# Chunked linear attention and a gated projection on one core: one visit of TensorE per unit, other PSUM banks, and signs by an AND

## The chip, the cores and the metric

The kernel runs on one core of a Trainium2 chip. The metric is device time in microseconds (us) from the start to the end of one execution. A core has TensorE (PE, with its weight load PEld), VectorE (DVE), ScalarE (ACT), GpSimd (POOL) and SyncE (SP), which issues the DMAs. A value that PE makes lands in one of eight PSUM banks.

## The reference

```python
def _attn_ref(q, k, v, alpha):                 # (4, 8, 768, 48)
    for t in range(S):
        state = alpha[:, :, t, :, None] * state + np.einsum('bhd,bhe->bhde', k[:, :, t], v[:, :, t])
        y[:, :, t] = np.einsum('bhd,bhde->bhe', q[:, :, t], state)
def _moe_ref(x, w_gate, w_val, w_out):         # x (3072, 384), d_ff 1536
    gate = 1.0 / (1.0 + np.exp(-(x @ w_gate)))
    return (gate * (x @ w_val) @ w_out)
```

A recurrence per batch and head with a decay per channel, and on its output, token by token, a sigmoid-gated two-matrix layer. All of it in float32.

## The kernel before, in words

**The dense part.** The 3072 tokens are six groups g of 512; each group takes 12 steps, one per 128 columns of the inner width, 72 steps s in all. To keep float32's accuracy a weight and an activation are each split into a high and a low part, and three products stand for one (`PAIRS`). A step has nine matmuls of 128x512 for the gate (into the bank `pg`), nine for the value (`pv`), and nine (`po`, three banks) which multiply the gated result of an earlier step by `w_out`: six with its high part `hh`, three with its low part `hl`. Between them ScalarE makes the sigmoid `sg` (L595), VectorE multiplies it into `pv` (L597), ScalarE casts that to `hh` (L599), and VectorE subtracts for `hl` (L600), which is the last reader of the `pv` bank.

**The attention part.** A unit u is one group of tokens and one pair of heads: 24 units, four per group. The first eight (`unit`) work in chunks of 128 tokens, the other sixteen (`late`) in chunks of 64. A late unit has on PE: four transposes of the decayed k (`turned`, L386, to `at`); the scores of 64x64 (`scores`, L526, two `at` banks); the products of k and v that are added to the state (`adds`, L533, the same two); and the outputs (`outputs`, L569, to `pg`). VectorE has two scans for the decays (L367, L371), the scaling of q (L515), the masks on the scores (L539, four per unit), eight state updates one after another (L552), and the subtract `yt` (L398) that splits the output; ScalarE copies the transposes to `kn` (L390) and casts the output (L397); GpSimd scales k (L374) and the states (`vs`, L557). The split output goes by DMA into `x`, the input of the next group's steps.

**The weights** come as 64-bit numbers and are cut into two float32 parts on the chip: for each of 25 pieces ScalarE scales the upper word (L333) and moves the top bits of the lower (L334), VectorE joins sign and bits by two `scalar_tensor_tensor` (L337), ScalarE casts (L339) and VectorE subtracts (L341). This and the eight early units fill the first part of the kernel.

**What sets the order.** `Plan` records every piece with its engine, an estimated time, a due step (`key`), and what it reads and writes; `order` then simulates the engines and takes, of the pieces that are ready, the one with the earliest due time. Instructions are issued in that order, engine by engine, and the tile framework adds the waits. Rings (`r_at`, `r_pg`, `r_pv`, `r_po`) hand out the banks in turn. For a late unit `begin` sets the due steps from `last_step`: transposes, scores, products and outputs have each their own.

Of the kernel before, what the change touches and what calls it, by code (L numbers as in the profile page):

```python
# [8 lines left out]
F32 = mybir.dt.float32  # L9
# [8 lines left out]
P = 128  # L18
# [206 lines left out]
def chunked(ctx, tc, rows, vc, vh, weights_in, out, const, ident, flags, weights, within):  # L225
# [67 lines left out]
    sb.tile([P, 104], F32, name="apart")  # L293
# [20 lines left out]
    plan.add("gpsimd", 1.5, NF - 4.0, later, writes=["later", *(("start", u) for u in range(EARLY))])  # L314
# [5 lines left out]
    def weight_piece(f, key):  # L320
        cuts = (0, DM, 2 * DM, WF) if f == 0 else (0, WF // 2, WF)
        over = before(f"w{f}") if f >= 6 else []
        for i, (lo, hi) in enumerate(zip(cuts, cuts[1:])):
# [4 lines left out]
            most = raw.bitcast(U16).rearrange("p m (w h) -> p m w h", h=2)[:, :, 0, 1]  # L328
# [83 lines left out]
    def unit(u, g, p, t):  # L412

        n, nch = T, CH
        bank = r_bank if u < NP else r_at
# [15 lines left out]
        (pkn, pk), *pas = bank.next(), bank.next(), bank.next()  # L431
# [47 lines left out]
        pyn, py = pas[0] if u < NP else r_pg.tiles[0]  # L479
# [15 lines left out]
    def late(u, g, p, t):  # L495
# [4 lines left out]
            out=tin[:, 0:A_Q], in_=rows[g, p, :, 0:A_Q]), writes=[(inn, m) for m in "ark"])  # L500
        (an, A), (vn, v), (vsn, vs) = r_A.next(), r_v.next(), r_vs.next()
        own = [slice(R * j, R * j + R) for j in range(2)]
        other = own[::-1]
        for j in range(2):
            plan.add("sync", (0.475, R * T * 4 / RATE), after(t["load"], 0.1), lambda j=j: nc.sync.dma_start(
                out=A[own[j], j], in_=rows[g, p, own[j], A_Q:WIDTH]), writes=[(an, 2 + j)])
        plan.add("sync", (0.475, P * CH * 2 * D * 4 / RATE), after(t["load"], 0.2), lambda: nc.sync.dma_start(
            out=v.rearrange("p c j e -> p (c j e)"), in_=vc[g, p]), writes=[(vn, "v")])
        for j in range(2):
            plan.add("sync", (0.475, R * EH * D * 4 / RATE), after(t["load"], 0.3), lambda j=j: nc.sync.dma_start(  # L510
                out=vs[other[j], j].rearrange("p c e -> p (c e)"), in_=vh[g, p, j]), writes=[(vsn, j)])
        kT = tin[:, A_K:A_Q]
        fn, F, decn, dec = decays(u, E, t, inn, tin)
# [4 lines left out]
        (pkn, pk), *pas = r_at.next(), r_at.next(), r_at.next()  # L518
# [111 lines left out]

    for i in range(WARM):
        warm(i)
# [192 lines left out]
```

## Time and profile before

| | us |
|---|---|
| median of 3 runs (lowest, highest) | 573.31 (571.58, 576.84) |
| the profiled execution | 573.71 |
| its span, first to last instruction | 571.6 |

The profile is of one execution. Times in its rows are from the start of the span; a large matmul's row (387 ns and more) overlaps the next one, so PE's pace is read from the chain of waits, where groups stand one behind another.

### The profile page before, as it was taken

The numbers are of one execution on the slowest core, as the hardware profiler recorded it, in microseconds if no ns is written. First come the engines' busy times: TensorE is split into PE (matmuls) and PEld (weight loads), VectorE is DVE, ScalarE is ACT, GpSimd is POOL, SyncE is SP. The second block draws the span as 40 slices with busy tenths as digits, with TensorE's granted clock in tenths as the row PEclk, the third lists the DMA queues.
The fourth block names the chain that finished last, engine by engine and source line by source line (L and its number), as shares of the span: only waits on it lengthen the run. The fifth ranks groups of instructions, "written<-read, shape, count | busy, mean of one in ns | idle before, by whom it ended". The sixth has DMA issues, their size and how long they took to land.

```text
span 571.6 us, 10275 instructions
## 1 busy us (share of the span) xinstructions
PE 553.7 (97%) x4150; PEld 434.1 (76%) x4150; DVE 335.2 (59%) x648; ACT 182.0 (32%) x331; POOL 93.3 (16%) x133
## 2 busy tenths in 40 slices
PE   8969999989999999999999999999999999999995
PEld 4657887767877777777777778777777878888884
DVE  7797989999753664754754844745748252221221
ACT  1556667653322222322212222213222212212121
POOL 6530212222210120220220210210202010000000
PEclk9988999999999999999999999999999999999999
DMA  8764775643412223312312332312332011100001
GB/s 316 255 190 154 249 214 177 192 140 106 153 49 79 60 74 84 122 56 80 90 52 61 112 108 60 106 57 61 92 127 61 1 29 29 55 1 0 3 0 60
DMA packets 21831, 55.90 MB, mean 98 GB/s; under 512 B 3472, under 2 KB 8592, under 8 KB 21776
## 3 DMA queue, kind: packets, MB, share of 16 engines
q1 hardware_dynamic: 21776, 55.17, 31.4%
q8 instruction: 34, 0.56, 0.4%
q14 instruction: 21, 0.17, 0.1%
HBM read 41.01 MB, written 4.72 MB: 80 GB/s over the span
## 4 chain that ended last, share of the span: by engine, by line
PE 89%; DVE 6%; issue 2%; DMA 1%; POOL 1%; ACT 0%; SPq 0%; DVEq 0%; POOLq 0%
PE pv L221 25%; PE po L608 25%; PE pg L221 25%; PE pg L569 3%; PE pv L580 2%; PE at L526 2%; PE at L386 1%; DMA x<-yt 1%; PE at L533 1%; PE at L438 1%; DVE st L552 1%; DVE raw L337 1%; DVE w L341 1%; DVE F L371 1%; PE pg L485 1%
## 5 line engine op out<-in xcount | busy, mean ns | idle before, releaser
L221 PE MATMUL pg<-x,w 128*128 128x512 f32 x648 | 162.8, 395 | 2.7 <-DMA x<-yt 2.7
L221 PE MATMUL pv<-x,w 128*128 128x512 f32 x648 | 162.2, 394 | 1.5 <-DVE hl L600 1.5
L221 PEld LDWEIGHTS pv<-x,w 128*128 128x128 f32 x648 | 120.1, 188 | 32.0 <-DVE hl L600 6.8
L221 PEld LDWEIGHTS pg<-x,w 128*128 128x128 f32 x648 | 120.5, 189 | 29.8 <-issue 3.1
L597 DVE TENSOR_TENSOR pv<-pv,sg 128x512 f32<-128x512 f32 x72 | 50.3, 699 | 122.2 <-PE pv L221 118.8
L608 PE MATMUL po<-hh,w 128*128 128x512 f32 x432 | 115.3, 395 | 0.1
L595 ACT ACTIVATE sg<-pg 128x512 f32<-128x512 f32 x72 | 43.1, 598 | 198.0 <-PE pg L221 108.2
L600 DVE TENSOR_TENSOR hl<-pv,hh 128x512 fp32r<-128x512 f32 x72 | 49.7, 690 | 84.5 <-PE po L608 69.9
L608 PEld LDWEIGHTS po<-hh,w 128*128 128x128 f32 x432 | 79.4, 188 | 16.6 <-ACT hh L599 0.5
L599 ACT CAST hh<-pv 128x512 fp32r<-128x512 f32 x72 | 42.1, 585 | 113.7 <-DVE pv L597 62.9
L608 PE MATMUL po<-hl,w 128*128 128x512 f32 x216 | 66.7, 406 | 0.0
L557 POOL TENSOR_TENSOR vs<-st,dec 64x384 f32<-64x384 f32 x32 | 26.9, 841 | 238.1 <-DVE st L552 218.2
L608 PEld LDWEIGHTS po<-hl,w 128*128 128x128 f32 x216 | 38.3, 188 | 8.5 <-issue 0.2
L374 POOL TENSOR_TENSOR in<-in,G 128x512 f32<-128x512 f32 x22 | 30.4, 1382 | 82.9 <-DVE G L367 30.3
L552 DVE SCALAR_TENSOR_TENSOR st<-st,dec,at 128x48 f32<-128x48 f32 x128 | 33.8, 264 | 7.9 <-PE at L533 2.9
L539 DVE TENSOR_TENSOR A<-at,mask 64x256 f32<-64x256 f32 x64 | 27.0, 422 | 1.5
L367 DVE TENSOR_TENSOR_SCAN G<-in,d1g 128x512 f32<-128x512 f32 x22 | 26.7, 1214 | 1.9 <-DMA in<-in_rows_dram 1.8
L371 DVE TENSOR_TENSOR_SCAN F<-in,d1f 128x512 f32<-128x512 f32 x22 | 27.6, 1253 | 0.1
L515 DVE TENSOR_TENSOR A<-A,F 64x512 f32<-64x512 f32 x32 | 22.7, 711 | 1.3 <-DMA A<-in_rows_dram 0.8
L569 PEld LDWEIGHTS pg<-A,vs 112*48 112x48 f32 (+1 forms) x512 | 16.8, 123 | 6.8 <-issue 6.8
L337 DVE SCALAR_TENSOR_TENSOR raw<-raw 128x576 uint32<-128x576 uint32 (+1 forms) x28 | 20.5, 747 | 0.0
L569 PE MATMUL pg<-A,vs 112*48 112x64 f32 (+1 forms) x512 | 18.8, 221 | 1.0 <-issue 0.4
(132 smaller groups left out, 391.1 us busy)
## 6 DMA issues: line engine op xcount, KB each, us to landing
in<-in_rows_dram SPq DMA_DIRECT2D x16, 516.5 KB, 3.7
raw<-in_w_dram SPq DMA_DIRECT2D x12, 576.0 KB, 4.6
x<-yt SPq DMA_DIRECT2D x35, 192.0 KB, 3.3
first_w<-in_w_dram SPq DMA_DIRECT2D x10, 576.0 KB, 4.7
out_dram<-raw SPq DMA_DIRECT2D x18, 256.0 KB, 2.5
v<-in_vc_dram SPq DMA_DIRECT2D x22, 192.0 KB, 3.5
A<-in_rows_dram SPq DMA_DIRECT2D x32, 128.0 KB, 2.7
in<-in_rows_dram SPq DMA_DIRECT2D x4, 772.5 KB, 5.0
```

Of the source, the lines that this page charges most:

```text
L221: nc.tensor.matmul(out=dst, lhsT=lhs(a, i), rhs=rhs(b, i), start=(n == 0 and i == 0), stop=(n == len(todo) - 1 and i == NK - 1))
L371: plan.add("vector", scan(n), after(t["G"], 0.01), lambda: nc.vector.tensor_tensor_scan(out=F, data0=az[:, 0:n], data1=d1f, initial=0.0, o ...
L374: plan.add("gpsimd", pool_(n), t["kt"], lambda: nc.gpsimd.tensor_tensor(out=kT, in0=kT, in1=G, op=ALU.mult), [gn, (inn, "r")], [(inn, "k")])
L539: plan.add("vector", vec(T // 2), t["mask"], lambda pa=pa, j=j, i=i: nc.vector.tensor_tensor(out=A[other[j], j].rearrange("p (c i t) -> p ...
L552: nc.vector.scalar_tensor_tensor(out=st[:, c + 1, :], in0=st[:, c, :], scalar=dec[:, c:c + 1], in1=pas[c % 2][1][:, T // 2 + c // 2 * D:T ...
L557: plan.add("gpsimd", pool_(EH * D), t["sd"], lambda j=j: nc.gpsimd.tensor_tensor(out=vs[own[j], j], in0=st[own[j], 0:EH], in1=dec[own[j]]. ...
L569: nc.tensor.matmul(out=py[R * j:R * j + D, cs], lhsT=vs[r, j, c, :], rhs=A[r, j, cs], start=True, stop=True)
L595: plan.add("scalar", act(T), None, lambda: nc.scalar.activation(out=sg, in_=got["g"][1][:, 0:T], func=AF.Sigmoid), [got["g"][0]], [sgn])
L597: plan.add("vector", vec(T), None, lambda: nc.vector.tensor_tensor(out=pv, in0=pv, in1=sg, op=ALU.mult), [sgn], [pvn])
L599: plan.add("scalar", act(T), None, lambda: nc.scalar.copy(out=hh, in_=pv), [pvn], [hhn])
L600: plan.add("vector", vec(T), None, lambda: nc.vector.tensor_tensor(out=hl, in0=pv, in1=hh, op=ALU.subtract), [pvn, hhn], [hln])
L608: nc.tensor.matmul(out=pso_now[m][1][:, 0:T], lhsT=weights.part("o", b, f)[:, m * P:(m + 1) * P], rhs=h[a][:, 0:T], start=(f == 0 and i == ...
```

## The change

The banks: `at` has two (before three), and one ring `gv` of three serves gate, value, the transposes and the outputs of the late units in turn (before one bank `pg` and one `pv`). The 64-chunk units: scores and products become one piece (`both`), and due steps from the new `visit` put it together with the outputs of the unit before and the transposes of the unit after; loads are due at other steps. In the weights the first of the two joins becomes a single-input AND on half words. The sigmoid and the operations behind it get due steps from step 12 on. In the last step the gate and value groups are due earlier, the output tiles are finished one after another, and the last is copied in two halves. Line numbers move: L526 to L530, L533 to L536, L569 to L576, L386 to L387, L398 to L399, L539 to L546, L552 to L559, L597 to L606, L600 to L608, L608 to L616.

```diff
-    r_at = ring("at", 3, 512, pool=ps)
-    r_pg, r_pv, r_po = ring("pg", 1, 512, pool=ps), ring("pv", 1, 512, pool=ps), ring("po", NM, 512, pool=ps)
-    r_bank = Ring([*r_at.tiles, *r_po.tiles, *r_pg.tiles])
+    r_at, r_gv, r_po = ring("at", 2, 512, pool=ps), ring("gv", 3, 512, pool=ps), ring("po", NM, 512, pool=ps)
+    r_bank = Ring([*r_at.tiles, *r_po.tiles, *r_gv.tiles[1:]])
...
-    plan.add("gpsimd", 1.5, NF - 4.0, later, writes=["later", *(("start", u) for u in range(EARLY))])
+    plan.add("gpsimd", 1.5, None, later, writes=["later", *(("start", u) for u in range(EARLY))])
...
-            for a, x, y in ((0x80000000, ALU.bitwise_and, ALU.bitwise_or), (3, ALU.logical_shift_left, ALU.bitwise_or)):
-                plan.add("vector", 0.07 + n / 860, kk, lambda upper=upper, lower=lower, a=a, x=x, y=y: nc.vector.scalar_tensor_tensor(
-                    out=lower, in0=upper, scalar=a, in1=lower, op0=x, op1=y), [ru], [rl], port=True)
+            plan.add("vector", 0.06 + n / 1920, kk, lambda most=most, sign=sign: nc.vector.tensor_scalar(
+                out=most, in0=sign, scalar1=0x8000, scalar2=None, op0=ALU.bitwise_and), [ru], [rl], port=True)
+            plan.add("vector", 0.07 + n / 960, kk, lambda upper=upper, lower=lower: nc.vector.scalar_tensor_tensor(
+                out=lower, in0=upper, scalar=3, in1=lower, op0=ALU.logical_shift_left, op1=ALU.bitwise_or), [ru], [rl], port=True)
...
-        (pkn, pk), *pas = bank.next(), bank.next(), bank.next()
+        (pkn, pk), *pas = [r_bank.next() for _ in range(3)] if u < NP else [r_gv.next(), r_at.next(), r_at.next()]
...
-        plan.add("tensor", (0.055 * EH + 0.15, 0.5), t["A"], scores, [(inn, "k"), (an, 2), (an, 3)], [x[0] for x in pas])
...
-        plan.add("tensor", (0.045 * EH, 0.5), t["Y"], adds, [knn, (vn, "v")], [x[0] for x in pas])
+        def both():
+            scores()
+            adds()
+
+        plan.add("tensor", (0.07 * EH + 0.062 * EH + 0.2, 0.5), t["A"], both, [(inn, "k"), (an, 2), (an, 3), knn, (vn, "v")], [x[0] for x in pas])
...
-        pyn, py = r_pg.tiles[0]
+        pyn, py = r_gv.next()
...
-        for nm, r, dt in (("g", r_pg, 0.0), ("v", r_pv, 0.33)):
-            pn, pt = r.next()
+        last = s == NG * NF - 1
+        for nm, dt in (("g", 0.0), ("v", 0.33)) if not last else (("g", -0.6), ("v", -0.5)):
+            pn, pt = r_gv.next()
...
+        first = (lambda x: s + x) if s >= NF else (lambda x: None)
+        plan.add("scalar", act(T), first(0.3), lambda: nc.scalar.activation(out=sg, in_=got["g"][1][:, 0:T], func=AF.Sigmoid), [got["g"][0]], [sgn])
...
-                plan.add("tensor", (MM * len(some), 1.0), s + 1 + 0.66 + 0.01 * m + 0.1 * some[0] - (0.5 if last else 0), lambda m=m, some=some: back(m, some),
+                at = s + 1 + (0.16 + 0.1 * m + 0.01 * some[0] if last else 0.66 + 0.01 * m + 0.1 * some[0])
+                plan.add("tensor", (MM * len(some), 1.0), at, lambda m=m, some=some: back(m, some),
...
+                cuts = ((0, T // 2), (T // 2, T)) if last and m == NM - 1 else ((0, T),)
...
-            o = last_step(u)
-            y = o - 3
-            t = dict(load=y - 5, G=y - 2.9, dec=y - 2, kt=y - 2.7, flag=y + 1 + 0.5 * p, q=y - 2.0, X=y - 0.50, A=y + 0.50, kn=y - 1,
-                     Y=y + 0.51, mask=y + 0.6, S=y + 0.55, sd=y + 0.7, out=o + 0.52, y=None)
+        y, x = visit(u), visit(u - 1)
+            t = dict(load=x - 2.5, G=x - 0.9, kt=x - 0.7, dec=x, kn=x + 0.6, more=y - 2.0, q=y - 1.0)
+        t.update(flag=y + 1 + 0.5 * p, X=after(x, 0.53), A=y + 0.5, mask=y + 0.6, S=y + 0.65, sd=y + 1.2, out=visit(u + 1) + 0.52, y=None)
```

The order of PE before, from one late unit's scores on, in the middle of the kernel. `at` are the banks of scores and products, `po` those of the output, `hl` and `w` the low part and the weights.

```order
L526 MATMUL at_119<-A_86,in_78 64x64
L526 MATMUL at_120<-A_86,in_78 64x64
L608 MATMUL po_123<-hl_117,w_639 128x512
L608 MATMUL po_124<-hl_117,w_639 128x512
L608 MATMUL po_125<-hl_117,w_639 128x512
L533 MATMUL at_119<-v_80,kn_84 48x48 x2
L533 MATMUL at_120<-v_80,kn_84 48x48 x2
```

The last of sixteen scores, then three matmuls of the dense part, then the products. Further on in the same period before, at the outputs and the transposes:

```order
L608 MATMUL po_125<-hh_114,w_695 128x512 x2
L608 MATMUL po_123<-hl_116,w_695 128x512
L569 MATMUL pg_121<-A_86,vs_88 48x64 x16
L608 MATMUL po_124<-hl_116,w_695 128x512
L608 MATMUL po_125<-hl_116,w_695 128x512
L386 MATMUL at_118<-ident,in_79 128x128 x4
L608 MATMUL po_123<-hh_115,w_763 128x512 x2
L221 MATMUL pv_122<-x_654,w_895 128x512 x9
```

The outputs cut the three `hl` matmuls apart, the transposes stand between `hl` and `hh`, and a value group follows. The order of PE after, at the same kind of unit:

```order
L536 MATMUL at_118<-v_81,kn_84 48x48 x2
L536 MATMUL at_119<-v_81,kn_84 48x48 x2
L576 MATMUL gv_121<-A_86,vs_88 48x64 x16
L387 MATMUL gv_122<-ident,in_78 128x128 x4
L616 MATMUL po_123<-hh_114,w_873 128x512 x2
L616 MATMUL po_124<-hh_114,w_873 128x512 x2
L616 MATMUL po_125<-hh_114,w_873 128x512 x2
L221 MATMUL gv_120<-x_718,w_1048 128x512 x9
```

The products (straight behind the scores, as the piece `both` is written), the outputs into one `gv` bank and the transposes into the next stand in one run, and only then the dense part goes on. VectorE before, from a unit's last mask on:

```order
L539 TENSOR_TENSOR A_87<-at_120,mask_104 64x4x64
L597 TENSOR_TENSOR pv_122<-pv_122,sg_112 128x512
L367 SCALAR_TENSOR_TENSOR G_91<-in_79,d1g_102 128x512
L369 TENSOR_TENSOR G_95<-G_91,tiny 128x8
L370 RECIPROCAL d1f<-G_95 128x8
L600 TENSOR_TENSOR hl_117<-pv_122,hh_115 128x512
L398 TENSOR_TENSOR yt_85<-pg_121,yt_85 128x512
L371 SCALAR_TENSOR_TENSOR F_93<-in_79,d1f 128x512
```

The subtract `yt` stands behind a scan and one `hl`; the unit's states and masks were ahead of all that, and belong to outputs not yet made. VectorE after, from the last value group before a visit on:

```order
L606 TENSOR_TENSOR gv_120<-gv_120,sg_112 128x512
L608 TENSOR_TENSOR hl_117<-gv_120,hh_115 128x512
L606 TENSOR_TENSOR gv_122<-gv_122,sg_112 128x512
L546 TENSOR_TENSOR A_86<-at_118,mask_104 64x4x64
L608 TENSOR_TENSOR hl_116<-gv_122,hh_114 128x512
L546 TENSOR_TENSOR A_86<-at_119,mask_104 64x4x64
```

and at the end of the same unit's eight state updates:

```order
L559 SCALAR_TENSOR_TENSOR st_109<-st_109,dec_98,at_119 128x48
L399 TENSOR_TENSOR yt_85<-gv_120,yt_85 128x512
L368 SCALAR_TENSOR_TENSOR G_90<-in_78,d1g_102 128x512
L606 TENSOR_TENSOR gv_120<-gv_120,sg_112 128x512
L608 TENSOR_TENSOR hl_117<-gv_120,hh_115 128x512
L517 TENSOR_TENSOR A_87<-A_87,F_93 64x512 x2
L370 TENSOR_TENSOR G_94<-G_90,tiny 128x8
```

Masks now come before the states, one `hl` stands between two masks, and the subtract `yt`, which empties the bank of the outputs, comes behind the last state update; the next scan and the next multiply follow it.

## Rows read from the trace of the kernel before

**Rows 1.** The page's first part: busy time, share of the span and number of instructions of each engine.

```profile
PE 553.7 (97%) x4150; PEld 434.1 (76%) x4150; DVE 335.2 (59%) x648; ACT 182.0 (32%) x331; POOL 93.3 (16%) x133
```

**Rows 2.** The chain of waits from 255 to 304 us, in order of time; columns: start, length in us, what (xN: that many instructions). One unit's period.

```profile
257.19 2.28 PE pv L221 x9
...
268.54 0.62 PE at L526 x32
269.17 0.90 PE po L608 x3
270.06 0.51 PE at L533 x32
270.57 2.28 PE pg L221 x9
272.85 2.04 PE pv L221 x9
...
276.48 0.05 issue
276.52 1.22 PE pg L569 x32
277.74 0.66 PE po L608 x2
278.40 0.44 PE at L386 x4
278.84 0.47 PE po L608 x2
279.30 2.28 PE pv L221 x9
```

**Rows 3.** The timeline of the same period, two places where PE's weight load waits and what ends the wait; columns: start, length in us, engine, line, operation, out<-in, count, and in brackets the idle time before and its releaser.

```profile
275.03 0.70 DVE L597 TENSOR_TENSOR pv<-pv,sg 128x512 f32<-128x512 f32 x1
275.82 0.60 ACT L595 ACTIVATE sg<-pg 128x512 f32<-128x512 f32 x1 [6.66 <-DVE pv L597]
...
276.49 1.10 PEld L569 LDWEIGHTS pg<-A,vs 128*48 128x48 f32 x32 [0.44 <-issue]
...
279.25 0.30 PEld L221 LDWEIGHTS pv<-x,w 128*128 128x128 f32 x2 [0.38 <-DVE hl L600]
```

**Rows 4.** The chain of waits, as in rows 2, at two other places, where two blocks of small matmuls stand side by side.

```profile
146.97 0.62 PE at L526 x32
147.59 1.03 PE pg L569 x32
148.63 2.27 PE pv L221 x9
...
456.27 0.62 PE at L526 x32
456.89 0.36 PE at L533 x32
457.25 2.26 PE pv L221 x9
```

**Rows 5.** Busy time by stretch; columns: from and to in us, length, then busy us and instructions of PE, its weight load, VectorE, ScalarE and GpSimd, the granted clock, the DMA engines' share and GB/s.

```profile
64.00:108.00 44.00, 44.00 (x289) 35.04 (x288) 40.14 (x68) 30.67 (x53) 9.83 (x10) 1.00 0.70 215
108.00:136.00 28.00, 24.54 (x214) 18.44 (x213) 27.04 (x49) 14.90 (x27) 9.80 (x12) 1.00 0.48 145
```

**Rows 6.** The timeline, columns as in rows 3: VectorE and ScalarE after one value group and at one unit (the first row follows the value group that the chain of waits has from 263.10 to 265.14); and one row of the page on DMA issues (operation, count, KB each, median us from issue to landing).

```profile
265.25 0.70 DVE L597 TENSOR_TENSOR pv<-pv,sg 128x512 f32<-128x512 f32 x1 [3.39 <-PE pv L221]
...
268.58 0.59 ACT L599 CAST hh<-pv 128x512 fp32r<-128x512 f32 x1 [0.76 <-PE po L608]
...
270.17 0.69 DVE L600 TENSOR_TENSOR hl<-pv,hh 128x512 fp32r<-128x512 f32 x1 [4.22 <-PE po L608]
...
270.78 2.42 DVE L552 SCALAR_TENSOR_TENSOR st<-st,dec,at 128x48 f32<-128x48 f32 x8
...
273.23 1.76 DVE L539 TENSOR_TENSOR A<-at,mask 64x256 f32<-64x256 f32 x4
...
279.12 0.68 DVE L398 TENSOR_TENSOR yt<-pg,yt 128x512 fp32r<-128x512 f32 x1
...
in<-in_rows_dram SPq DMA_DIRECT2D x16, 516.5 KB, 3.7
```

**Rows 7.** The timeline of PE at one place after 433 us.

```profile
443.24 2.34 PE L221 MATMUL pv<-x,w 128*128 128x512 f32 x9 [0.47 <-DVE hl L600]
```

**Rows 8.** Groups by line of the weight conversion and of one small operation; columns: line, engine, operation, shapes, count, busy us, mean ns of one, idle us before and releaser.

```profile
L337 DVE SCALAR_TENSOR_TENSOR raw<-raw 128x576 uint32<-128x576 uint32 (+1 forms) x28 | 20.5, 747 | 0.0
L333 ACT ACTIVATE raw<-raw 128x576 f32<-128x576 f32 (+1 forms) x14 | 10.1, 721 | 9.2 <-DMA raw<-in_w_dram 9.1
L334 ACT ACTIVATE raw<-raw 128x576 uint32<-128x576 uint16 (+1 forms) x14 | 9.9, 710 | 0.0
L677 DVE TENSOR_SCALAR within<-at 1x1 int32<-1x1 f32 x1 | 0.1, 145 | 0.0
```

**Rows 9.** The timeline of the end of the kernel.

```profile
564.33 1.07 ACT L623 COPY raw<-po 128x512 f32<-128x512 f32 x2 [2.24 <-PE po L608]
564.56 0.69 DVE L621 COPY raw<-po 128x512 f32<-128x512 f32 x1 [1.74 <-PE po L608]
564.95 1.58 SPq L624 DMA_DIRECT2D out_dram<-raw  x3
```

More of the change, by code (lines that the diff above doesn't have):

```diff
@@ L477, in unit @@
         yield
-        pyn, py = pas[0] if u < NP else r_pg.tiles[0]
+        pyn, py = pas[0] if u < NP else r_gv.next()
         def outputs():
@@ L517, in late @@
         bound(u, t, fn, F)
-        (pkn, pk), *pas = r_at.next(), r_at.next(), r_at.next()
-        knn, kn = turn(t, inn, kT, pkn, pk)
+        yield
+        pas = [r_at.next(), r_at.next()]
         def scores():
@@ L547, in late @@
         done = EH if u >= EARLY + NP else CH
-        plan.add("gpsimd", 0.28, t["G"], lambda: nc.gpsimd.tensor_copy(out=st[:, 0, :], in_=st[:, done, :]), writes=[sn])
+        plan.add("gpsimd", 0.28, t["S"], lambda: nc.gpsimd.tensor_copy(out=st[:, 0, :], in_=st[:, done, :]), writes=[sn])
         def states():
@@ L569, in outputs @@
                     nc.tensor.matmul(out=py[R * j:R * j + D, cs], lhsT=vs[r, j, c, :], rhs=A[r, j, cs], start=True, stop=True)
-        plan.add("tensor", (0.055 * 2 * EH + 0.1, 0.5), t["out"], outputs, [(vsn, x) for x in range(4)] + [(an, x) for x in range(4)], [pyn])
+        plan.add("tensor", (0.07 * 2 * EH + 0.05, 0.5), t["out"], outputs, [(vsn, x) for x in range(4)] + [(an, x) for x in range(4)], [pyn])
         finish(g, p, t, pyn, py)
     wz = ident.bitcast(BF16)[:, 0:P]
-    banks = [*r_at.tiles, *r_po.tiles, *r_pg.tiles, *r_pv.tiles]
+    banks = [*r_at.tiles, *r_po.tiles, *r_gv.tiles[1:], r_gv.tiles[0]]
     def warm(i):
@@ L632, in chunked, with last_step, visit @@
         warm(i)
+    def last_step(u):
+        return (1, 3, 5, 7)[u - NP]
+    def visit(u):
+        return NF * (u // NP - 1) + 7 - 3 * (NP - 1 - u % NP)
     def begin(u):
@@ L653, in chunked @@
         weight_piece(f, None)
-    now = begin(NP)
+    visits = {visit(u): u for u in range(EARLY, n_units + 1)}
+    finished = {last_step(u): u for u in range(NP, EARLY)}
+    now, following = begin(NP), None
     next(now), next(now)
-    finished = {last_step(u): u for u in range(NP, NG * NP)}
     for s in range(NG * NF):
@@ L660, in chunked @@
             u = finished[s]
-            following = begin(u + 1) if u + 1 < NG * NP else iter((None, None))
-            next(following)
+            then = begin(u + 1)
+            next(then)
             next(now, None)
-            next(following)
-            now = following
+            if u + 1 < EARLY:
+                next(then)
+                now = then
+            else:
+                now, following = iter(()), then
+        if s in visits:
+            u = visits[s]
+            next(following, None)
+            next(now, None)
+            now, following = following, begin(u + 1) if u + 1 < n_units else iter(())
+            next(following, None)
+            next(now, None)
     every, one, total = sb.tile([P, 1], F32, name="every"), sb.tile([P, 1], F32, name="one"), r_at.next()
     nc.vector.memset(one, 1.0)
-    late, n_units = NG * NF - 4, NG * NP
+    late = NG * NF - 4
     plan.add("scalar", 0.5, late, lambda: nc.scalar.activation(out=starts.rearrange("p u c -> p (u c)"), in_=starts.rearrange("p u c -> p (u c)"),
```

54 lines of the change are left out of this document (30 added, 24 removed).

## The prediction

> **What bounds the kernel now.** I began with the page's line on the engines [rows 1]: PE is busy in 553.7 of 571.6 us, so only work taken off PE, or a wait that PE makes, can move the time. The chain of waits says what PE does in that time. In the second half it repeats one pattern every 22.11 us (257.19 to 279.30) [rows 2], and one such period carries three steps of the dense part and one 64-chunk unit. A group of nine large matmuls takes 2.04 us, 0.2267 us each; three steps are 81 of them, 18.36 us. The other 3.75 us are the unit, and the rows show what they are: four blocks of small matmuls in four places. The scores (L526) take 0.62, and the three large ones after them 0.90 in place of 0.68: 0.22 more. The products with v (L533) take 0.51 and the group after them 0.24 more. The outputs (L569) take 1.22 with 0.05 of issue ahead and 0.21 more behind. The transposes (L386) take 0.44 and 0.02 more behind. The next pv group is 0.24 too long. Sum 3.77, against 3.75 measured.
>
> So every block of narrow matmuls costs about 0.22 us when PE goes back to full-width ones, and the transposes, full-width themselves, do not. Where two blocks happen to adjoin [rows 4], this is paid once: scores and products are 0.62 + 0.36 and then 2.26, scores and outputs 0.62 + 1.03 and then 2.27. The products alone took 0.51 and the outputs alone 1.22, so next to another block they are 0.15 and 0.19 shorter besides.
>
> Two of the extras are not PE's own [rows 3]. The outputs' weight load starts at 276.49, 0.07 after the sigmoid ended (275.82 + 0.60): their tile is the one pg bank, held until the sigmoid has read it, and the sigmoid stood behind a multiply that VectorE began only at 275.03. And the pv group's weight load waits 0.38 for the subtract L600, which is what empties the one pv bank.
>
> In the first half VectorE is the rival bound [rows 5]: from 64 to 108 us PE is never idle, but from 108 to 136 us VectorE is busy in 27.04 of 28 us and PE in 24.54. Those 3.46 us are the only large gap before the tail.
>
> **Part 1, one visit.** In the changed program 14 of the 16 late units have scores, products, the outputs of the unit before and the transposes of the next in one run on PE. The first unit has only its transposes apart; the last has no transposes, and its outputs come alone. From the rows where blocks adjoin: 0.62 + 0.36 + 1.03, the transposes 0.44, and one return of 0.24: 2.69 us in place of 3.75, 1.06 saved. No row has transposes right behind the outputs. If the return is paid at neither place the visit is 2.45, if at both, 2.93; I take once, since two adjoining blocks [rows 4] show no gap between them.
>
> **Part 2, three banks in turn.** Gate, value, transposes and outputs now take three banks one after another, and the unit itself two. What does each wait for? The outputs take the value bank of the step before last, empty for over a step; the transposes take the gate bank just read, whose sigmoid had a whole value group (2.04 us) to end in. The two waits of [rows 3] go, which is contained in the 1.06. The wait that is new: the second group after the visit takes the outputs' bank, and the subtract L399 that frees it now stands on VectorE behind four masks and eight state updates. Counting from the end of the last value group before the visit, with durations of [rows 6]: multiply from 0.11 (265.14 to 265.25) to 0.81; one mask 0.44, from when the products are out (0.98), to 1.42; the cast on ScalarE 0.59, done by 1.43; its subtract 0.69, to 2.15; three masks, 1.31, to 3.46; states 2.42, to 5.88; L399 0.68, to 6.56. PE asks for the bank after the visit's 2.45, six large ones with their return (1.60), a group (2.04) and three more (0.68): 6.77 in the chain's ends, and some 0.16 earlier in starts: 6.61. So the wait is 0.05 us short of being felt. I take 0.1 us, bounds 0 and 0.4. Behind L399 in VectorE's queue stand the next scan and multiply, which PE needs only a step later, so a late L399 costs that bank alone. On SyncE's queue the scan's load now goes out once the scores have read its buffer, about 0.8 after the visit's start, and lands 3.7 later [rows 6], 2 us before the scan's turn; the other loads follow it and are wanted a step later. GpSimd's products for the outputs (L557) have a whole period. All this costs nothing; a scan held up would hold the multiply behind it, which PE asks for some 8 us after the scan's turn.
>
> **Sum of the late part.** Twelve whole periods at 0.96 are 11.5 us. The other four units, at both ends of the late part, have blocks that adjoin already [rows 4]; I take half a us each, 2.0. Together 13.5; bounds 6 (2.93 and 0.4 for a wait) and 18 (2.45 and none). One more stall goes: at 443.24 a pv group starts 0.47 us late behind L600 [rows 7], with its restart 0.6.
>
> **Part 3, signs by an AND.** Of the 50 instructions on line L337 (two for each of 25 weight pieces [rows 8]) 25 become a single-input AND over as many half words. On the trace no single-input operation of this size between SBUF tiles is to be seen on VectorE. Bounds: 0.15 us (the tensor_scalar L677 on one element, all fixed cost) and 0.75, what an L337 costs. ScalarE reads the same half words as fast as words (L334 710 ns, L333 721), so the stride is not dear to read; writing half words has no row. The nearest row is L337 itself, so I take 0.70 us: 25 x 0.05, about 1 us of VectorE. The Trainium skill (VectorE: DVE Perf Modes, "What auto-detection actually checks") says that a single-source operation whose source and destination lie in SBUF, with even outer dimensions, is run at two results per cycle, and pairs of 16-bit values only at unit step. By that page's table an estimate is (58 + 576/2) / 0.96 = 360 ns for this AND, 25 x 0.39 = 9.7 us off VectorE, and the kernel would come to about 555 us; no run here shows it.
>
> **Early part as a whole.** The 3.46 us of idle PE are what VectorE's relief and the new order of its queue can give, and no more. With 1 us of relief I take half, 1.7. The other bound is a loss: transposes and outputs of the early units now sit in the banks that the gate and value groups need, and these are emptied by a VectorE that is 97% busy. Four early units after 45 us, about 1 us each: 4 lost.
>
> **Part 4, the end.** Now the last step finishes its three output tiles one after another, and the last is copied in halves by two engines. Before [rows 9], two copies on ScalarE end at 564.33 + 1.07 = 565.40, and the three transfers are issued from 564.95 to 566.53. The middle tile's copy starts at 564.56, so the last tile is ready one large matmul later, 564.8. An operation on 256 elements of PSUM costs 0.44 (four masks in 1.76 [rows 6]), so both halves are out near 565.2, and two issues of 0.53 follow: 566.3. I take 0.2 us; bounds 0 and 0.9. The first writes on GpSimd keep their place, so they cost nothing.
>
> **Sum.** 13.5 + 0.6 + 1.7 + 0.2 = 16.0 us. From the profiled execution's 573.71 that leaves 557.7; that run is 0.4 above the median of 573.31, so 557 us.
>
> **Rivals.**
> - *The AND runs two elements per cycle.* Of L337's 0.747 us, 576 elements at one per cycle are 0.60 and 0.15 is fixed; half of 0.60 makes 0.45, 25 x 0.30 = 7.5 us off VectorE, and all 3.46 us of idle PE go: 1.8 more than forecast, 555 us. For it speaks the full VectorE queue; against it no row. It is the rule of the page named above. Chance 0.22.
> - *The outputs' bank comes late in each period.* If masks, states and L399 end 0.6 us later than I count, 14 visits x 0.6 = 8.4 are given back: 565.5 us. The narrow margin speaks for it; that VectorE has 13 us of work in a 21 us period speaks against more. Chance 0.13.
> - *Early sharing of banks.* PE waits 4 us in the early units and the 1.7 gained is not: 16.0 - 5.7 = 10.3, 563 us. Chance 0.17.
> - *Slower: writing half words is dear.* If an AND takes 1.7 us, 25 x 0.95 = 24 us come onto VectorE where it is the bound, and the kernel ends 24 - 16 = 8 us later, 581 us. It decides from 0.747 + 16.0/25 = 1.4 us on. Only the missing row speaks for it. Chance 0.04.
> - *The change doesn't do what it says*, the visit costing what the four blocks did: the late part stays, some 571 us. The order of instructions and [rows 4] speak against it. Chance 0.04.
>
> **How the numbers follow.** The forecast itself has 0.40, own range 553 to 561. A measurement of this kernel can tell about 1% (5.7 us) from no change. Faster by more than that are the forecast, the first three rivals but for a tail of 0.01: 0.91. Within it, the last rival and that tail: 0.05. Slower: 0.04. The range runs from 552 (visit 2.45 us, no wait, all idle time gone) to 566 (the bank late), which leaves out the last two rivals and the extremes of the others.
>
> **What would show it.** In the profile after: periods near 21.1 us in the late half; one small-block run of about 2.4 us with one return of 0.24; no wait of the outputs on the sigmoid; PE waiting for L399 by 0 to 0.2 us; the AND's mean as a row of its own; PE idle between 100 and 140 us at about half of 3.46; the last transfer issued some 0.2 us earlier after PE's end. The prediction is wrong if periods stay above 21.6 us, or if PE has new gaps behind VectorE before 150 us.

## The result, and the profile of the changed kernel

The changed kernel takes 560.4 us (median of 4 runs, 559.28 to 561.48), against 573.5 for the kernel before beside it (571.58 to 576.84): a ratio of 0.976, 95% interval 0.974 to 0.979. The forecast was 557.0 with a range of 552 to 566. The span of the profiled execution went from 571.6 to 558.2 us, 13.4 less where the sum said 16.0.

One period of the late half, in the chain of waits (start, length in us, what):

```profile
256.06 0.62 PE at L530 x32
256.69 0.36 PE at L536 x32
257.05 1.03 PE gv L576 x32
258.08 0.59 PE gv L387 x4
258.67 1.38 PE po L616 x6
260.05 2.04 PE gv L221 x9
...
262.77 2.06 PE gv L221 x9
...
277.07 0.62 PE at L530 x32
```

From scores to scores it is 21.01 us, in [rows 2] it was 22.11: 1.10 gained where the sum had 0.96. The visit is 0.62 + 0.36 + 1.03 + 0.59 and 0.02 in the six large ones behind it, 2.62 against 2.69 forecast. The transposes (0.59 in place of 0.44) pay for the return to full width; nothing behind them does. The group at 262.77 takes the outputs' bank, and the timeline (with the idle time before and its releaser in brackets) shows how close that is:

```profile
261.72 0.68 DVE L399 TENSOR_TENSOR yt<-gv,yt 128x512 fp32r<-128x512 f32 x1
...
262.45 0.81 PEld L221 LDWEIGHTS gv<-x,w 128*128 128x128 f32 x4
```

L399 ends at 262.40 and the weight load starts at 262.45, in time but for 0.02.

L399 is felt at a second place, which the forecast did not have. The split output goes by DMA into `x`, the input of the next group of tokens, and at the last unit of a group PE wants it at once. The chain of waits there:

```profile
303.72 0.70 DVE yt L399
...
305.02 3.61 DMA x<-yt
...
308.77 1.84 PE gv L221 x7
```

PE's matmul at 308.77 starts 0.30 us late, and two others like it (at 224 and 393 us) 0.24 and 0.11 late; in the kernel before no such wait is to be seen after 168 us.

The loss is at the end of the early part. First the stretch of 100 to 140 us, then that of [rows 5], then two pieces of it, by busy time (from and to, length, busy us of PE, its weight load, VectorE, ScalarE and GpSimd, then granted clock, DMA share and GB/s); behind them the timeline there:

```profile
100.00:140.00 40.00, 36.00 (x233) 27.76 (x232) 38.25 (x65) 23.25 (x40) 6.00 (x7) 0.96 0.49 145
108.00:136.00 28.00, 24.55 (x170) 19.24 (x167) 26.29 (x47) 16.05 (x30) 4.18 (x5) 0.98 0.47 144
131.00:134.50 3.50, 0.41 (x2) 0.00 (x0) 2.78 (x6) 0.58 (x2) 2.23 (x3) 1.00 0.00 0
134.50:139.50 5.00, 4.94 (x15) 3.92 (x16) 4.93 (x8) 1.24 (x3) 1.82 (x2) 0.66 0.00 0
```

```profile
127.92 1.73 DVE L546 TENSOR_TENSOR A<-at,mask 64x256 f32<-64x256 f32 x4
...
129.21 2.21 PE L221 MATMUL gv<-x,w 128*128 128x512 f32 x9
129.66 2.37 DVE L559 SCALAR_TENSOR_TENSOR st<-st,dec,at 128x48 f32<-128x48 f32 x8
131.81 2.08 POOL L564 TENSOR_TENSOR vs<-st,dec 64x384 f32<-64x384 f32 x2 [21.81 <-DVE st L559]
131.94 1.35 DVE L336 TENSOR_SCALAR raw<-raw 128x576 uint16<-128x576 uint16 x1
133.10 0.78 DVE L606 TENSOR_TENSOR gv<-gv,sg 128x512 f32<-128x512 f32 x1
133.92 0.59 ACT L607 CAST hh<-gv 128x512 fp32r<-128x512 f32 x1 [4.37 <-DVE gv L606]
...
134.56 2.65 PE L616 MATMUL po<-hh,w 128*128 128x512 f32 x6 [3.15 <-ACT hh L607]
```

From 108 to 136 us PE is idle for 3.45 us, as before, but now nearly all of it in one piece of 3.15; from 100 to 140 us it is idle for 4.00, where it was 3.46. At 131 PE wants `hh`, and VectorE is doing four masks, eight state updates and one AND before the multiply that `hh` comes from. After the stall PE runs at a granted clock of 0.66 for 5 us, which is 1.2 GHz for about two thirds of them; by 5 x 0.34 that is an estimate of 1.7 us lost. In the kernel before, the longest wait of PE in that stretch was 1.2 us (us in all, times, longest), and the clock stayed at 1.00 [rows 5]:

```profile
PE at L438 <- POOL in L426: 1.2, 1, 1.2
```

To split the 13.4 us I added up, over all of PE's large matmuls, how much longer than 0.2267 us it was from one's start to the next one's (what is not dense work at full pace, in us). After 168 us that is 51.9 before and 39.1 after; up to there 35.4 and 35.0, but before that point the old kernel had also done one unit's outputs (1.3) that the new one had still to do. So the late part gave 12.9 + 1.3 = **14.2 us** (forecast 13.5 + 0.6), the early part **lost 1.0** (forecast a gain of 1.7), and the end gave some 0.2.

### The profile page after: what moved, and what is told of

It is laid out like the page before. It is cut to its first block, busy times and chain, and to the rows that moved or that the text cites. A ratio compares the mean times of both kernels' runs of the same rounds, so it can differ in the third digit from the quotient of the medians.

```text
span 558.2 us, 10252 instructions
## 1 busy us (share of the span) xinstructions
PE 541.1 (97%) x4150; PEld 435.2 (78%) x4150; DVE 338.8 (61%) x649; ACT 183.6 (33%) x331; POOL 104.8 (19%) x133
## 4 chain that ended last, share of the span: by engine, by line
PE 82%; DVE 11%; DMA 3%; issue 1%; ACT 0%; SPq 0%; POOL 0%; DVEq 0%; POOLq 0%; ACTq 0%
PE gv L221 47%; PE po L616 23%; DMA x<-yt 3%; PE gv L576 3%; PE gv L587 2%; DVE w L342 2%; PE gv L387 2%; PE at L530 2%; DVE raw L336 1%; DVE raw L338 1%; PE at L536 1%; DVE F L372 1%; DVE gv L606 1%; DVE st L559 1%; DVE yt L399 1%
## 5 line engine op out<-in xcount | busy, mean ns | idle before, releaser
L221 PE MATMUL gv<-x,w 128*128 128x512 f32 x1296 | 319.7, 393 | 3.2 <-DMA x<-yt 2.4
L221 PEld LDWEIGHTS gv<-x,w 128*128 128x128 f32 x1296 | 243.2, 189 | 58.2 <-issue 4.4
L606 DVE TENSOR_TENSOR gv<-gv,sg 128x512 f32<-128x512 f32 x72 | 50.4, 700 | 161.3 <-PE gv L221 160.1
L616 PE MATMUL po<-hh,w 128*128 128x512 f32 x432 | 114.0, 398 | 3.1 <-ACT hh L607 3.1
L607 ACT CAST hh<-gv 128x512 fp32r<-128x512 f32 x72 | 42.3, 587 | 171.1 <-DVE gv L606 165.5
L616 PEld LDWEIGHTS po<-hh,w 128*128 128x128 f32 x432 | 79.8, 189 | 19.6 <-ACT hh L607 3.6
L564 POOL TENSOR_TENSOR vs<-st,dec 64x384 f32<-64x384 f32 x32 | 36.8, 1150 | 277.2 <-DVE st L559 276.0
L604 ACT ACTIVATE sg<-gv 128x512 f32<-128x512 f32 x72 | 43.0, 597 | 114.5 <-PE gv L221 108.4
L608 DVE TENSOR_TENSOR hl<-gv,hh 128x512 fp32r<-128x512 f32 x72 | 49.8, 692 | 30.9 <-ACT hh L607 29.0
L616 PE MATMUL po<-hl,w 128*128 128x512 f32 x216 | 61.7, 391 | 0.0
L616 PEld LDWEIGHTS po<-hl,w 128*128 128x128 f32 x216 | 40.3, 188 | 8.2
L559 DVE SCALAR_TENSOR_TENSOR st<-st,dec,at 128x48 f32<-128x48 f32 x128 | 33.9, 265 | 4.2
L546 DVE TENSOR_TENSOR A<-at,mask 64x256 f32<-64x256 f32 x64 | 26.8, 419 | 3.7 <-PE at L536 3.2
L380 ACT ACTIVATE F<-F 128x512 f32<-128x512 f32 x23 | 14.5, 632 | 27.2 <-DVE A L517 25.3
L576 PE MATMUL gv<-A,vs 128*48 128x64 f32 (+1 forms) x512 | 17.6, 221 | 0.0
L576 PEld LDWEIGHTS gv<-A,vs 128*48 128x48 f32 (+1 forms) x512 | 15.2, 123 | 1.2 <-issue 0.4
L398 ACT CAST yt<-gv 128x512 fp32r<-128x512 f32 x20 | 11.7, 587 | 10.3 <-PE gv L576 9.9
L587 PE MATMUL gv<-ident 128*128 128x512 bf16 x55 | 14.1, 396 | 0.0
```

Of the source, the lines that this page charges most:

```text
L221: nc.tensor.matmul(out=dst, lhsT=lhs(a, i), rhs=rhs(b, i), start=(n == 0 and i == 0), stop=(n == len(todo) - 1 and i == NK - 1))
L559: nc.vector.scalar_tensor_tensor(out=st[:, c + 1, :], in0=st[:, c, :], scalar=dec[:, c:c + 1], in1=pas[c % 2][1][:, T // 2 + c // 2 * D:T ...
L564: plan.add("gpsimd", pool_(EH * D), t["sd"], lambda j=j: nc.gpsimd.tensor_tensor(out=vs[own[j], j], in0=st[own[j], 0:EH], in1=dec[own[j]]. ...
L576: nc.tensor.matmul(out=py[R * j:R * j + D, cs], lhsT=vs[r, j, c, :], rhs=A[r, j, cs], start=True, stop=True)
L604: plan.add("scalar", act(T), first(0.3), lambda: nc.scalar.activation(out=sg, in_=got["g"][1][:, 0:T], func=AF.Sigmoid), [got["g"][0]], [sgn])
L606: plan.add("vector", vec(T), first(0.4), lambda: nc.vector.tensor_tensor(out=pv, in0=pv, in1=sg, op=ALU.mult), [sgn], [pvn])
```

## The experiments

The theories: **theory 1**, VectorE simply has too much work before 136 us, and the AND adds to it or takes too little away; **theory 2**, the order of VectorE's queue makes the stall. Two further questions were whether the late gain comes from the returns or from the banks, and how much room L399 has.

The variants that leave the visits alone differ from the changed kernel only in the early part: from the gate group of step 16 to PE's end they take 384.7 to 385.1 us. So one number of the trace tells them apart besides the median: the start of that group, counted from the first gate matmul. In the changed kernel it is 130.2 us. In tail_whole below, which differs from it only at the very end, it is 129.4, so I read nothing from differences under 1 us.

### The AND taken back: old_join

```diff
-            plan.add("vector", 0.06 + n / 1920, kk, lambda most=most, sign=sign: nc.vector.tensor_scalar(
-                out=most, in0=sign, scalar1=0x8000, scalar2=None, op0=ALU.bitwise_and), [ru], [rl], port=True)
+            plan.add("vector", 0.06 + n / 1920, kk, lambda upper=upper, lower=lower: nc.vector.scalar_tensor_tensor(
+                out=lower, in0=upper, scalar=0x80000000, in1=lower, op0=ALU.bitwise_and, op1=ALU.bitwise_or), [ru], [rl], port=True)
```

> The changed kernel with the AND taken back to the old two-input join; the planner's costs stay as they are, so every engine has the same order. Theory 1 (the AND's own time): its mean of 0.82 us free of GpSimd stands against 0.75 for the join, 25 x 0.07 = 1.7 us of VectorE in a part where it is the bound; taking it back gives 1 to 2 us, 558.5 to 559.5 us. Theory 2 (the place in the queue): the 3.3 us stall of PE at 131 us is there because the multiply L606 stands behind four masks, eight state updates and one join, whatever the join is; only the 0.6 by which that one AND ran long beside GpSimd can come back, and with it some of the half-clock time after the stall: 559.5 to 560.4 us, and a stall of 2.5 us or more stays. Rival (the AND is faster than the join): 561 us or more.

Measured: 560.5 us (ratio 0.977, 0.974 to 0.980), step 16 at 129.3, and the stall is as long as in the changed kernel:

```profile
131.62 1.30 DVE L336 SCALAR_TENSOR_TENSOR raw<-raw 128x576 uint32<-128x576 uint32 x1
132.85 0.69 DVE L606 TENSOR_TENSOR gv<-gv,sg 128x512 f32<-128x512 f32 x1
133.57 0.58 ACT L607 CAST hh<-gv 128x512 fp32r<-128x512 f32 x1 [4.34 <-DVE gv L606]
...
134.20 2.03 PE L616 MATMUL po<-hh,w 128*128 128x512 f32 x5 [3.12 <-ACT hh L607]
```

The join beside GpSimd takes 1.30 as the AND took 1.35, so theory 2's extra 0.6 was not there either. Theory 2 stands for this stall, and the AND is neither gain nor loss that can be seen in the time. The 0.82 against 0.75 in the expectation was a misreading: a row's length is not how long the engine is kept. From the start of an AND to the start of the next instruction it is 0.607 us (median of 22), from that of a join 0.669 (median of 40 in the kernel before).

### The planner told the AND's time: true_cost

```diff
-            plan.add("vector", 0.06 + n / 1920, kk, lambda most=most, sign=sign: nc.vector.tensor_scalar(
+            plan.add("vector", 0.15 + n / 860, kk, lambda most=most, sign=sign: nc.vector.tensor_scalar(
```

> The changed kernel with one number of the planner altered: the AND is reckoned at 0.15 + n/860 (0.82 us for 576) in place of 0.06 + n/1920 (0.36). The instructions are the same, their order is not. Theory 2 (the planner's wrong price sets the order that makes the stall at 131 us): the multiply that PE waits for comes ahead of a unit's states or of a join, the 3.3 us stall and the 2.2 us at the half clock after it go for the most part: 555 to 557.5 us. Theory 1 (VectorE is simply full until 136 us, by 1.7 us more than before): the stalls change place and the sum stays, 559.5 to 561.5 us.

Measured: 559.4 us (ratio 0.975, 0.972 to 0.977), step 16 at 128.8. Stalls of 1.92, 0.98, 0.98 and 1.17 us, from 95 to 133 us, stand in place of the one of 3.31. Inside the bounds of the changed kernel, as theory 1 said: a better price for one operation orders the whole part anew, and does not by itself put first what PE wants.

### One multiply moved: mult_first

```diff
...
+        at = row.index(self.masks[0])
+        n = next(x for x in row[at:] if x in self.multiplies)
+        row.remove(n)
+        at = max(at, 1 + max(row.index(x) for x in self.parts[n][4]))
+        row.insert(at, n)
...
```

> The changed kernel with one VectorE instruction moved: the multiply L606 that PE waits for at 131 us goes ahead of the four masks and eight state updates of the first late unit; nothing else moves. Theory 2 (the place of that one instruction makes the stall): the 3.3 us stall and the 2.2 us at the half clock behind it go, and VectorE, which has 11 us to spare from 136 to 168 us, catches up with the masks and states: 555 to 556.5 us. Theory 1 (VectorE is full, so what is moved ahead delays something else that PE needs): a stall of the same size comes later, before 150 us, 559.5 to 561 us.

Measured: **556.9 us** (ratio 0.970, 0.967 to 0.973), 3.5 us less than the changed kernel and the best of all. Step 16 at 127.7. The same place in its timeline:

```profile
129.08 0.69 DVE L614 TENSOR_TENSOR gv<-gv,sg 128x512 f32<-128x512 f32 x1
...
130.50 2.21 PE L227 MATMUL gv<-x,w 128*128 128x512 f32 x9
130.72 0.59 ACT L615 CAST hh<-gv 128x512 fp32r<-128x512 f32 x1
131.55 2.36 DVE L566 SCALAR_TENSOR_TENSOR st<-st,dec,at 128x48 f32<-128x48 f32 x8
...
132.55 1.52 PE L624 MATMUL po<-hh,w 128*128 128x512 f32 x6
```

`hh` is ready at 131.3, before PE has finished the group ahead, and the six matmuls take 1.52 in place of 2.65. The stall and the half clock are gone; 1.05 and 0.83 us of shorter stalls come at 136 and 142, so a part of what theory 1 said holds too. By the same sum over the large matmuls the early part is now 32.5 in place of 35.0, a gain on the kernel before of 35.4 - 32.5 - 1.3 = 1.6. One instruction in the wrong place cost about as much as the prediction missed by.

### The masks moved instead: masks_later, masks_later_old

```diff
...
+        at, end = row.index(self.masks[0]), 1 + row.index(self.last_weight)
+        later = {*self.masks[:4], self.states[0]}
...
+        return (row[:at] + [n for n in row[at:end] if n not in later]
+                + [n for n in row[at:end] if n in later] + row[end:])
...
```

> The changed kernel with the four masks and eight state updates of the first late unit put behind the last weight piece on VectorE (its AND, join and subtract), the multiply L606, one low part and one scan; what depends on them goes with them, and nothing else moves. Theory (in this stretch VectorE's queue serves work that is wanted 15 us later ahead of work that PE wants now): both the 3.3 us stall at 131 us with its half clock and the two shorter ones that moving the multiply alone left at 136 and 142 us (1.05 and 0.83, behind the last weight piece) go: 554 to 556 us. Rival (the outputs of that unit, whose masks and scaled states are now 5 us later, become the next thing that PE waits for, at the visit near 150 us): 557 to 560 us.

> As the kernel with the masks later, and with the AND taken back to the old two-input join in the same places. The join is shorter by 0.07 us, 25 x 0.07 = 1.7 us less for VectorE. If VectorE's sum of work up to 136 us sets the time once the order is right, 0.5 to 1.5 us less than that kernel; if not, the same within 0.5 us. If the AND pays off in this order after all, more than that kernel.

Measured: 561.0 us (ratio 0.976, 0.974 to 0.978) and 561.1 (0.976, 0.974 to 0.979). The theory fell, and not by the rival's mechanism: the stall is 3.1 us again, 9 us later, behind the next multiply, which now has masks, states and a scan ahead of it (the timeline of masks_later, and the busy time behind the stall):

```profile
142.65 0.58 ACT L617 CAST hh<-gv 128x512 fp32r<-128x512 f32 x1
...
143.29 1.22 PE L626 MATMUL po<-hh,w 128*128 128x512 f32 x2 [3.13 <-ACT hh L617]
```

```profile
143.30:150.20 6.90, 6.90 (x19) 5.50 (x20) 2.65 (x4) 1.76 (x3) 0.00 (x0) 0.59 0.27 102
```

The low clock lasts longer here, 0.59 for 6.9 us. In both kernels PE waits 3.1 us for a multiply that has this block of 4.1 us ahead of it; in mult_first, where the block comes right behind a multiply, the waits were 1.05 and 0.83. That masks_later and masks_later_old agree shows once more that join or AND is the same in the time.

### The sign on other engines and in other forms: and_forms, and_pool, act_sign, mix_sign

```diff
...
+                **(dict(out=raw.bitcast(U16).rearrange("p m h -> p (m h)")[:, 0:n], in0=raw.bitcast(U16).rearrange("p m h -> p (m h)")[:, 2 * n:3 * n]) if f % 3 == 1 else
+                   dict(out=lower, in0=upper) if f % 3 == 2 else dict(out=most, in0=sign)),
...
```

> The disputed cost by itself: of the weight pieces one third keep the AND as it is (half words at a stride of four), one third do it on as many half words that lie side by side, one third on whole words at a stride of two; the values of the weights are wrong in two thirds. If the stride of the half words is what keeps the AND from two elements per cycle, the second form takes 0.45 us or less for 576 elements and the others 0.75 to 0.82; if a single-input operation between SBUF tiles is at two per cycle in words too, the third takes 0.45; if neither, all three stand between 0.70 and 0.85.

The rows of VectorE, one of each form with the instruction behind it (whole words; half words at a stride; half words side by side):

```profile
55.06 0.47 DVE L336 TENSOR_SCALAR first_w<-first_w 128x576 uint32<-128x576 uint32 x1
55.43 0.69 DVE L453 TENSOR_TENSOR A<-at,mask 128x512 f32<-128x512 f32 x1
...
57.30 0.82 DVE L336 TENSOR_SCALAR raw<-raw 128x576 uint16<-128x576 uint16 x1
57.91 0.24 DVE L468 SCALAR_TENSOR_TENSOR st<-st,dec,gv 128x48 f32<-128x48 f32 x1
...
116.73 0.28 DVE L336 TENSOR_SCALAR raw<-raw 128x576 uint16<-128x576 uint16 x1
116.93 0.68 DVE L610 TENSOR_TENSOR hl<-gv,hh 128x512 fp32r<-128x512 f32 x1
```

From start to next start 0.37, 0.61 and 0.20 us. So a single-input operation between SBUF tiles runs at nearly twice the pace of the join on whole words (0.37 against 0.67), and faster still on half words side by side, but not on half words at a stride. The Trainium skill (VectorE: DVE Perf Modes, "What auto-detection actually checks") says two results per cycle for one source in SBUF and a destination in SBUF, with even or equal outer dimensions. The whole words agree with that; the half words at a stride meet these conditions too, and there the measured 0.61 us decides against the estimate of 0.36. With 16 of the ANDs faster, 5 us less for VectorE, the one run took 557.45 us and the stall 1.94, which speaks for less work helping as well.

and_pool writes the sign by a comparison on GpSimd:

```diff
-            plan.add("vector", 0.06 + n / 1920, kk, lambda most=most, sign=sign: nc.vector.tensor_scalar(
-                out=most, in0=sign, scalar1=0x8000, scalar2=None, op0=ALU.bitwise_and), [ru], [rl], port=True)
+            plan.add("gpsimd", 0.1 + n / 440, kk, lambda most=most, sign=sign: nc.gpsimd.tensor_scalar(
+                out=most, in0=sign, scalar1=32768.0, scalar2=32768.0, op0=ALU.is_ge, op1=ALU.mult), [ru], [rl])
```

> The changed kernel with the 25 sign instructions on GpSimd in place of VectorE, as a comparison (half word at least 32768) times 32768, and the planner told so. It takes 25 x 0.73 = 18 us off VectorE before 136 us. Theory 1 (the amount of VectorE's work bounds the early part): the early stalls go, 3.3 + 2.2 us and some of the shorter waits, 553 to 556 us. Rival (GpSimd is slow at it, 1.4 us or more each as its other instructions on 512 elements, and what it runs beside VectorE's slows both, as the join of 1.30 us did): conversion is no faster, 560 to 565 us.

> The changed kernel with the sign made by ScalarE: it multiplies the upper word by 0.0 and writes the result as bfloat16 into the upper half of the lower word, so that only the sign bit is left there (minus zero); the planner is told so. VectorE loses 25 x 0.73 = 18 us before 136 us, ScalarE gains 25 x 0.63 = 16 us and goes from 65 to 81 of the 100 us from 36 to 136. Theory 1 (VectorE's amount of work bounds the early part): the 3.3 us stall, the half clock behind it and some of the shorter waits go, 552 to 556 us. Rival (PE then waits for ScalarE, whose sigmoids and casts stand behind the sign moves): 557 to 561 us.

> As the kernel with the sign made by ScalarE, but so only for the odd steps' weights; for the even ones VectorE multiplies the upper word by 0.0 and writes bfloat16 into the half word, a single-input operation that reads whole words and writes half words. If reading half words at a stride is what slows the AND, this takes about 0.45 us for 576 elements, as the form on whole words did; if writing them does, 0.75 to 0.85. The time: by theory 1, 9 to 13 us come off VectorE, 553 to 557 us; by the rival, 557 to 560 us.

act_sign, and the odd steps' weights of mix_sign:

```diff
+            plan.add("scalar", act(n), kk, lambda most=most, upper=upper: nc.scalar.activation(
+                out=most.bitcast(BF16), in_=upper.bitcast(F32), func=AF.Copy, scale=0.0), [ru], [rl])
```

Measured: and_pool 574.2 us (ratio 1.000, 0.998 to 1.002), act_sign 562.0 (0.980, 0.978 to 0.983), mix_sign 560.7 (0.977, 0.975 to 0.979); in the last two the weights come out with wrong values, though every operation is done. None gained. The same write is dearer on GpSimd and on ScalarE, and for mix_sign as dear on VectorE: these are the groups by line of the three, in that order (count, busy us, mean ns).

```profile
L336 POOL TENSOR_SCALAR raw<-raw 128x576 uint16<-128x576 uint16 x12 | 37.4, 3113 | 12.0 <-ACT raw L334 12.0
```

```profile
L336 ACT ACTIVATE raw<-raw 128x576 bf16<-128x576 f32 x12 | 18.2, 1513 | 0.2
L334 ACT ACTIVATE raw<-raw 128x576 uint32<-128x576 uint16 x12 | 8.8, 730 | 0.0
```

```profile
L340 DVE TENSOR_SCALAR raw<-raw 128x576 bf16<-128x576 f32 x5 | 4.1, 817 | 0.0
```

mix_sign answers its question: with whole words read and half words written the row is 0.82 again, so writing is what costs. On ScalarE that write takes 1.51, while reading half words (L334) takes 0.73. act_sign was no clean test of theory 1: VectorE's busy time from 36 to 136 us fell from 94.3 to 79.9 us, but ScalarE's rose from 65.3 to 90.0.

### The price of a visit: out_apart, twice

```diff
...
+        next(parked, None)
+        parked = iter(())
...
             next(following, None)
-            next(now, None)
+            parked = now
...
```

> The changed kernel with the outputs of a late unit taken out of the visit and done about one step later, alone; scores, products and transposes stay together, the three banks in turn too. Theory of the prediction (each separate place costs a return and the block is longer alone): per unit 0.24 + 0.19, times 14 units about 6 us: 566 to 567.5 us, periods of 21.4 to 21.5 us in place of 21.0. Rival (the gain comes from the banks, whose waits are gone here too): within 1 us of 560.4.

In this kernel the scaled q of a unit is overwritten before the outputs have read it; all operations are done. Measured: 563.2 us (ratio 0.980, 0.976 to 0.984), and in the chain:

```profile
265.11 1.03 PE gv L576 x32
266.14 1.58 PE po L616 x6
...
272.49 1.36 PE po L616 x6
```

The period is 21.22, 0.21 more, all of it the return (1.58 against 1.36). Over 14 units that is 2.9 us, and the medians differ by 2.8. Between these two traces it is less: from step 16 to PE's end 386.8 against 384.7 us, 2.1 more, in part because the three waits for `x` are not there. The time lies between the two expectations: a place of its own costs the return and no more. The outputs alone take 1.03, as in the visit. So of the 1.22 in [rows 2], 0.19 was not the price of standing alone, as I had it; the rows leave the wait for the one bank [rows 3].

```diff
...
+        def split():
+            for _ in range(2 if g * NP + p >= EARLY else 1):
+                nc.vector.tensor_tensor(out=yt[:, 1], in0=py[:, 0:T], in1=yt[:, 0], op=ALU.subtract)
...
```

> The changed kernel with the subtract L399 of the late units done twice over, so that the outputs' bank comes free 0.69 us later and VectorE has 0.69 us more to do in each period. Theory of the prediction (L399 ends just in time, margin 0.05 to 0.2 us): PE waits 0.5 to 0.65 us in 14 visits, 7 to 9 us: 567 to 569.5 us. Rival (VectorE has some 8 us to spare in a period and PE's order hides it): within 1 us of 560.4.

Measured: 571.6 us (ratio 0.994, 0.992 to 0.997). PE waits 0.58 us or more in each of 14 visits:

```profile
268.05 0.69 DVE yt L401
268.77 0.70 DVE yt L401
...
269.52 2.37 PE gv L221 x9
```

That is 8.5 us. With the slower restart behind it the period is 21.74 us, 0.73 more than in the changed kernel, and from step 16 to PE's end the trace takes 394.6 in place of 384.7 us, 9.9 more; the medians differ by 11.2. L399 was put off by some 0.7 us and PE waits 0.58, so the margin was real and about 0.1 us wide: with it nearly all of the gain stands or falls.

This run shows something else. Its early part is ordered as in the changed kernel, and the stall is there, 3.12 us long, but no half clock follows it (the six matmuls behind it in the chain of waits, and the busy time there):

```profile
138.55 1.67 PE po L619 x6
```

```profile
138.50:143.50 5.00, 4.95 (x22) 4.06 (x23) 4.93 (x8) 1.23 (x2) 1.83 (x2) 1.00 0.00 0
```

The granted clock is 1.00 where the changed kernel had 0.66, and in and_forms it was 0.66 for 5 us behind a stall of only 1.94. So the 1.7 us of clock do not come with every stall, nor only with the longest; what decides it is open.

### The last tile whole: tail_whole

```diff
-                cuts = ((0, T // 2), (T // 2, T)) if last and m == NM - 1 else ((0, T),)
+                cuts = ((0, T),)
```

> The changed kernel with the last output tile copied and sent whole by ScalarE, in place of two halves on ScalarE and VectorE. In the changed kernel the second half waited 0.40 us for the first, so the two came out 0.87 us after PE's last matmul. Theory (the halves run one after the other, so halving gains nothing): one copy of 0.59 us, the last transfer issued 0.2 to 0.3 us earlier, and from PE's end to the span's end 6.4 to 6.7 us in place of 6.68. Rival (the smaller last transfer lands sooner, which pays for it): 6.8 to 7.0 us.

One run, 559.5 us. The last copies of the changed kernel, and of this one:

```profile
551.56 0.37 ACT L635 COPY raw<-po 128x256 f32<-128x256 f32 x1 [0.77 <-PE po L616]
551.97 0.42 DVE L632 COPY raw<-po 128x256 f32<-128x256 f32 x1 [0.40 <-ACT raw L635]
```

```profile
550.68 0.58 ACT L635 COPY raw<-po 128x512 f32<-128x512 f32 x1 [0.77 <-PE po L616]
```

The halves come one after the other (VectorE's copy waits for ScalarE's), the second 0.87 us after PE's last matmul; the whole tile is out 0.61 after it. But its transfer of 256 KB takes 4.1 us from issue to landing, the half's 3.2, and from PE's end to the span's end it is 7.01 in place of 6.69 us. That is the rival's range. That the smaller transfer is the reason is not shown: in the kernel before, a whole last tile landed after 3.07 us, and each of these is one transfer of one execution.

## Why the prediction came out as it did

- **Late part, right.** 14.2 us measured, 14.1 forecast; the period 21.01 against 21.15. Three returns of 0.21 to 0.24, the waits on two banks, and some of the small blocks' own length are what went. Of these out_apart tested one return, 0.21; the others are read from the rows, and the new banks were not tried with the old visits. The split was wrong in one place: the outputs' 0.19 was not the price of standing alone. It did not touch the sum, since both went.
- **The wait for L399, right.** 0.02 us, inside the bounds of 0 and 0.4. The three waits for `x` behind it, 0.1 to 0.3 us each, were not in the sum. Its rival (565.5 us) was near: doubling the subtract gave 571.6.
- **The AND, right in size, in part by luck.** 0.05 us each was forecast, 0.06 measured from start to start; by the length of the row, which the forecast went by, the AND is longer than the join (0.82 against 0.75). The rival of two elements per cycle fell, and so did the slower one (1.7 us); the cause, that half words are written at a stride, no row of before could show.
- **The early part, wrong.** "With 1 us of relief I take half, 1.7" took idle PE as something that shrinks with VectorE's sum of work. The relief came and the idle time stayed, 3.45 us, nearly all in one stall behind a block of masks and states, and the granted clock of 0.66 after it cost some 1.7 us more. So the early part lost 1.0 where it was to gain 1.7, which is most of the 3.4 us that the forecast was short. Two of the forecast's own signs spoke against it: between 100 and 140 us PE is idle for 4.00 us and not for half of 3.46, and there is a new gap behind VectorE before 150 us, by which the prediction was to be called wrong. The total came out inside the range because the late part, which was right, is by far the largest term. mult_first shows that the order makes this stall: with one multiply in another place the kernel takes 556.9 us, and the early part gains 1.6. The loss of 1.0 is within the bound of 4, but that bound was put down to shared banks, and at this stall PE waits for a cast, not for a bank; how much the sharing costs elsewhere was not tried alone.
- **The end, right in size, not in the way.** 0.2 us forecast; from PE's end to the last landing it is 4.22 in place of 4.43, to the span's end 6.69 in place of 6.88. But the forecast had both halves out some 0.4 us after PE, side by side, and they came one after the other, the second at 0.87.

## What to carry to other kernels

Where two engines take turns, count the stalls of the bound one by its queue's order, not by its sum of work: a long block in front of a short operation that another engine waits for can cost nearly the block's length, and the clock may fall behind the stall besides (0.66 for 5 us here, 1.00 behind the same stall in twice). Price an operation from the start of its row to the start of the next, and from rows with the same stride on the side that is written.

## What the hardware showed that I had not expected

Writing half words at a stride takes longer than writing as many words: for 576 elements 1.25 us from start to start on ScalarE (L336 in act_sign) against 0.63 (L333 and L334 in the changed kernel), and 0.60 on VectorE (mix_sign) against 0.37 (and_forms). On ScalarE no run writes half words side by side, so there it is not shown whether the stride or the two bytes make it. GpSimd's product L564 takes longer beside VectorE's scan: the second of a unit's two takes 1.63 us where it begins 0.23 us behind the scan's start, and 0.83 in the kernel before, where masks run beside it; the group's mean is 1150 ns against 841. It has a whole period, so that cost nothing.
